# A chunked attention and a wave MLP: two stages in sequence, and the same work woven by pairs of batches

## The chip, the cores and the metric

The kernel runs on one core of a Trainium2 chip. Its engines have instruction queues of their own: TensorE (PE, and PEld for its weight loads) for matmuls and transposes, VectorE (DVE), ScalarE (ACT), GpSimd (POOL) and SyncE (SP). POOL issues the transfers that load the inputs, SP those that store the output; both run on the same 16 DMA engines. The metric is the device time of one execution in microseconds (us), and a version's time is the median of its runs.

## What is computed

```python
# q, k, v: (8, 8, 576, 64); w_theta, w_ch: (512, 512); w_tok_r, w_tok_i: (576, 576); float32
q_c, k_c, v_c = (t.reshape(B, H, 9, 64, D) for t in (q, k, v))      # chunks of 64 tokens
attn = softmax(q_c @ k_c.T / sqrt(64))                              # inside a chunk only
x = (attn @ v_c) -> (B, S, H * D)                                   # (8, 576, 512)
theta = x @ w_theta
zr, zi = x * cos(theta), x * sin(theta)
y[b] = w_tok_r @ zr[b] + w_tok_i @ zi[b]                            # over the tokens of a batch
u = x + y
out = u + maximum(u @ w_ch, 0.0)
```

The softmax's subtraction of the row's maximum leaves its value unchanged; both kernels leave it out. Inputs become 16-bit floats (f16) as they are loaded, sums are 32-bit, the output is 32-bit.

## The kernel before

A batch has 576 tokens: four tiles of 128 and one of 64 (`SB_SZ`). In every loop over tiles the fifth pass works on half a tile.

**Weights.** POOL loads `w_theta` and `w_ch` as they are; both token weights are loaded and then transposed on TensorE (line 78, 25 blocks each), since the token mix contracts over the tokens.

**Attention, a loop over 8 batches.** POOL issues 15 loads a batch (line 107): q, k and v for each of 5 tiles, 128 KB each as written, 64 KB for the half tile; the buffers hold two batches. q and k are transposed per tile and pair of heads (line 120) and copied out by DVE (lines 127, 130). Per head, TensorE computes 9 blocks of 64x64 scores (line 142), ACT takes the exponential of the first eight and the ninth chunk in two instructions (lines 147, 153), and 9 matmuls with a column of ones give the row sums (line 161). Then values times weights (line 180), and DVE multiplies by the reciprocal sums (lines 167, 185) into `x16`, of which there is one for each batch.

**MoE part, a second loop over 8 batches.** x is transposed (line 202; ACT copies, line 207), theta is computed per tile (line 219), ACT takes cosine and sine (lines 226, 230), DVE the products zr and zi (lines 234, 237). The token mix takes the transposed token weights as the stationary and z as the moving operand, so that its result `ps_y` has tokens on the partitions: 5 output tiles of 10 matmuls each, 512 columns wide (line 251). DVE adds x (line 259). u is transposed again (line 269; ACT copies, line 274), multiplied with `w_ch` (line 282), and DVE computes max(., 0) + u in one instruction (line 290) into one of two output buffers, which SP stores.

All PSUM tiles come from one pool of 8 buffers, one bank each. The framework's scheduler chooses each engine's order from the program's order and from what is ready.

## Time and profile before

| | |
|---|---|
| runs | 331.72 us median of 3 (331.07 to 333.35) |
| span of the profiled execution | 329.0 us |
| median of the runs less that span | 2.7 us |
| TensorE busy (x matmuls) | 285.2 us (x3138) |
| DVE, ACT, POOL busy | 146.2, 115.7, 105.4 us |
| loads | 120 issues for q, k, v; 16.54 MB written in all by POOL's queue |
| stores | 40 issues, 9.44 MB |

An instruction's busy time runs from its start to its modelled end, and matmuls overlap: the sum of busy times is no measure of the pace. The pace is the time from one start to the next. In the slices of the page each digit is a share in tenths; PEclk is the granted clock of TensorE, where 9 stands for the full one. A load's size in the profile is what it writes (16-bit); it reads twice as much.

### The profile page before, as it was taken

How to read it: one execution, taken by the hardware profiler on the slowest of the kernel's cores; microseconds unless marked ns; L12 is line 12 of the kernel's file. 1: busy time of each engine (PE TensorE's matmuls, PEld its weight loads, DVE VectorE, ACT ScalarE, POOL GpSimd, SP SyncE). 2: the span in 40 equal slices, each digit the busy share in tenths (PEclk: the TensorE clock that was granted, in tenths of full speed). 3: DMA queues.
4: the chain of work that ended last, by engine and by line, in shares of the span. 5: the costliest groups of instructions: out<-in, count | busy, mean ns of one | idle time of the engine just before them, and what ended most of it. 6: DMA issues, size and time to landing. Idle time of an engine off the chain costs nothing.

```text
span 329.0 us, 7260 instructions
## 1 busy us (share of the span) xinstructions
PE 285.2 (87%) x3138; PEld 159.2 (48%) x3138; DVE 146.2 (44%) x319; ACT 115.7 (35%) x290; POOL 105.4 (32%) x132
## 2 busy tenths in 40 slices
PE   0328977879869889999999999999999999999992
PEld 0216866768858777334344344344344344344340
DVE  0216437357347354544534625525535534533532
ACT  0001440431421424805615515425426326227220
POOL 8189999999999900000000000000000000000000
PEclk9999577575676576999999999999999999999998
DMA  6999999999999980003003004004004003003004
GB/s 107 175 134 152 146 138 138 149 142 140 151 138 144 147 44 3 2 0 130 16 0 131 16 0 140 5 0 145 0 0 146 0 0 131 14 1 129 15 1 144
DMA packets 120064, 26.44 MB, mean 80 GB/s; under 512 B 113248, under 2 KB 115424, under 8 KB 120032
## 3 DMA queue, kind: packets, MB, share of 16 engines
q0 software_dynamic: 114784, 16.54, 79.4%
q1 hardware_dynamic: 5248, 9.44, 8.4%
q8 instruction: 24, 0.39, 0.5%
q14 instruction: 8, 0.07, 0.1%
HBM read 33.06 MB, written 9.44 MB: 129 GB/s over the span
## 4 chain that ended last, share of the span: by engine, by line
PE 62%; POOL 14%; DMA 12%; DVE 7%; issue 2%; ACT 1%; DVEq 0%; POOLq 0%; ACTq 0%
PE ps_y L251 30%; POOL qk L107 9%; PE ps_theta L219 8%; PE ps_uw L282 8%; DMA out_dram<-o 5%; POOL v L107 5%; DMA wtok_nat<-in_moe_w_tok_r_dram 3%; PE ps_uT L269 3%; PE ps_sT L142 3%; PE ps_xT L202 2%; PE ps_rs L161 2%; PE ps_wtokT L78 2%; DVE o L290 2%; DMA wtok_nat<-in_moe_w_tok_i_dram 2%; DMA qk<-in_q_dram 2%
## 5 line engine op out<-in xcount | busy, mean ns | idle before, releaser
L251 PE MATMUL ps_y<-zr,wtokTr 128*128 128x512 f16 (+3 forms) x200 | 53.9, 382 | 0.7 <-DVE zr L234 0.6
L251 PE MATMUL ps_y<-zi,wtokTi 128*128 128x512 f16 (+3 forms) x200 | 54.5, 384 | 0.0
L259 DVE TENSOR_TENSOR u<-ps_y,x 128x512 f16<-128x512 f32 (+1 forms) x40 | 27.6, 690 | 53.6 <-PE ps_y L251 53.6
L147 ACT ACTIVATE eT<-ps_sT 128x256 f16<-128x256 f32 x64 | 24.4, 382 | 69.5 <-PE ps_sT L142 66.7
L274 ACT COPY uT<-ps_uT 128x512 f16<-128x512 f16 (+1 forms) x40 | 18.6, 564 | 82.3 <-PE ps_uT L269 82.3
L290 DVE SCALAR_TENSOR_TENSOR o<-ps_uw,u 128x512 f32<-128x512 f32 (+1 forms) x40 | 27.6, 690 | 40.0 <-DMA out_dram<-o 22.5
L107 POOL DMA_DIRECT2D v<-in_v_dram x40 | 37.3, 933 | 1.5 <-DMA wch<-in_moe_w_ch_dram 1.3
L107 POOL DMA_DIRECT2D qk<-in_q_dram x40 | 37.3, 933 | 1.2 <-issue 0.8
L219 PE MATMUL ps_theta<-wtheta,xT 128*128 128x512 f16 (+1 forms) x160 | 36.9, 381 | 0.7 <-ACT xT L207 0.7
L107 POOL DMA_DIRECT2D qk<-in_k_dram x40 | 37.3, 932 | 0.1
L282 PE MATMUL ps_uw<-wch,uT 128*128 128x512 f16 (+1 forms) x160 | 36.9, 381 | 0.0
L251 PEld LDWEIGHTS <-wtokTi 128*128 128x128 f16 (+3 forms) x200 | 16.5, 99 | 38.5 <-issue 29.3
L120 PE MATMUL ps_qkT<-id,qk 128*128 128x128 f16 (+1 forms) x320 | 29.9, 267 | 5.8 <-DMA qk<-in_q_dram 4.5
L142 PE MATMUL ps_sT<-qT,kT 64*64 64x64 f16 x576 | 30.1, 232 | 3.7 <-DVE kT L130 3.6
L251 PEld LDWEIGHTS <-wtokTr 128*128 128x128 f16 (+3 forms) x200 | 17.8, 99 | 31.9 <-issue 17.0
L161 PE MATMUL ps_rs<-ones,eT 64*64 64x1 f16 x576 | 26.9, 191 | 7.0 <-ACT eT L147 7.0
L120 PEld LDWEIGHTS <-qk 128*128 128x128 f16 (+1 forms) x320 | 26.1, 127 | 8.7 <-DMA qk<-in_q_dram 6.1
L230 ACT ACTIVATE sin<-ps_theta,zerob 128x512 f16<-128x512 f32 (+1 forms) x40 | 29.6, 741 | 0.0
L226 ACT ACTIVATE cos<-ps_theta,pihalf 128x512 f16<-128x512 f32 (+1 forms) x40 | 29.5, 737 | 0.0
L207 ACT COPY xT<-ps_xT 128x512 f16<-128x512 f16 (+1 forms) x40 | 18.6, 564 | 28.2 <-PE ps_xT L202 28.2
L161 PEld LDWEIGHTS <-eT 64*64 64x64 f16 x576 | 21.8, 144 | 11.1 <-ACT eT L147 8.9
L185 DVE TENSOR_TENSOR x<-ps_xout,recip 128x512 f16<-128x512 f32 (+1 forms) x40 | 24.6, 681 | 0.4
(39 smaller groups left out, 242.2 us busy)
## 6 DMA issues: line engine op xcount, KB each, us to landing
out_dram<-o SPq DMA_DIRECT2D x32, 256.0 KB, 2.0
qk<-in_q_dram POOLq DMA_DIRECT2D x32, 128.0 KB, 5.5
qk<-in_k_dram POOLq DMA_DIRECT2D x32, 128.0 KB, 5.8
v<-in_v_dram POOLq DMA_DIRECT2D x32, 128.0 KB, 5.8
out_dram<-o SPq DMA_DIRECT2D x8, 128.0 KB, 2.3
wtok_nat<-in_moe_w_tok_r_dram POOLq DMA_DIRECT2D x1, 576.0 KB, 10.0
wtok_nat<-in_moe_w_tok_i_dram POOLq DMA_DIRECT2D x1, 576.0 KB, 6.1
wtheta<-in_moe_w_theta_dram POOLq DMA_DIRECT2D x1, 512.0 KB, 6.1
```

Source lines behind the costliest of these rows:

```text
L107: nc.gpsimd.dma_start(dst, t_ap[b, :, sb * P : sb * P + ns, :].rearrange("h s d -> s h d"),)
L120: nc.tensor.transpose(pqk[:, which, e, 0:ns], qk16[0:ns, sb, which, 2 * e : 2 * e + 2, :].rearrange("s h d -> s (h d)"), id16[0:ns, 0:ns],)
L142: nc.tensor.matmul(pst[cp * CH : cp * CH + CH, cb, :], kT[par * D : par * D + D, e, sl], qT[par * D : par * D + D, e, sl],)
L161: nc.tensor.matmul(ps_rs[cp * CH : cp * CH + CH, cb, h : h + 1], eT[cp * CH : cp * CH + CH, h, cb, :], ones16[cp * CH : cp * CH + CH, :],)
L185: nc.vector.tensor_tensor(out=x16[b][0:ns, sb, :].rearrange("s (h d) -> s h d", h=H), in0=psx[0:ns], in1=recip[0:ns, sb, :].unsqueeze(-1). ...
L219: nc.tensor.matmul(pth[0:ns], xT[:, db, sb * P : sb * P + ns], wtheta16[:, db, :], start=(db == 0), stop=(db == NDB - 1),)
L226: nc.scalar.activation(out=cos16[0:ns, sb, :], in_=pth[0:ns], func=AF.Sin, bias=pihalf[0:ns], scale=1.0,)
L230: nc.scalar.activation(out=sin16[0:ns, sb, :], in_=pth[0:ns], func=AF.Sin, bias=zerob[0:ns], scale=1.0,)
L251: nc.tensor.matmul(psy[0:nt], wT[0:ns, sb, tsl], z[0:ns, sb, :], start=(step == 0), stop=(step == nsteps - 1),)
L259: nc.vector.tensor_tensor(out=u16[0:nt, mt, :], in0=psy[0:nt], in1=x16[b][0:nt, mt, :], op=ALU.add,)
L282: nc.tensor.matmul(puw[0:nt], uT[:, db, mt * P : mt * P + nt], wch16[:, db, :], start=(db == 0), stop=(db == NDB - 1),)
L290: nc.vector.scalar_tensor_tensor(out=o32[0:nt], in0=puw[0:nt], scalar=0.0, in1=u16[0:nt, mt, :], op0=ALU.max, op1=ALU.add,)
```

## The change

Two batches are one pair of 1152 tokens, that is 9 full tiles; tile 4 (`MID`) holds the last 64 tokens of the first and the first 64 of the second batch. `GROUPS` puts the 9 tiles into steps of 2, 2, 1, 2 and 2. A PSUM tile is now two banks, and there are 4 of them.

- The loads for tile 4 go in two halves. q and k have 6 buffers of one tile, v has room for two pairs, with a 65th column of ones behind each head.
- `a1` transposes q and k (one DVE copy a group), `a2` computes scores (one exponential a group), `a3` multiplies with values and ones at once, so that the row sum comes out as the 65th column, `a4` transposes x, `a5` computes theta, cosine, sine and the products. For tile 4, half of zr and zi is exchanged between partitions by two transfers that SP issues, so that one tile holds both parts of one batch.
- `y` is the token mix transposed: z is the stationary operand and the token weights move, 288 columns at a time, 18 matmuls for each of 4 channel blocks of a batch. Its result has channels on the partitions, and DVE adds the transposed x: this is already the transposed u. The token weights are transposed twice (`tok_w`): for the first batch of a pair, and for the second with rows shifted by 64.
- `w` multiplies by `w_ch`, and by the identity to get u back in its natural layout; ACT takes the relu, DVE the sum, SP stores. The output has 4 buffers.
- The order is written out (`manual_schedule`): each engine takes its instructions in the program's order. `weave` spreads the steps of a second list evenly between those of a first. While pair p goes through `y` and `w`, pair p + 1 goes through `a1` to `a5`, and POOL issues its loads.

The core of the diff; what it removes are the two loops above.

```diff
+def weave(main, filler):
+    n, m = len(main), len(filler)
+    done = 0
+    for i, step in enumerate(main):
+        step()
+        want = ((i + 1) * m) // n
+        while done < want:
+            filler[done]()
+            done += 1
...
-    psum = ctx.enter_context(tc.tile_pool(name="psum", bufs=8, space=bass.MemoryType.PSUM))
+    GROUPS = [(0, 2), (2, 2), (4, 1), (5, 2), (7, 2)]
+    psum = ctx.enter_context(
+        tc.tile_pool(name="psum", bufs=4, space=bass.MemoryType.PSUM)
+    )
+    nat = ctx.enter_context(tc.tile_pool(name="nat", bufs=6))
+    ctx.enter_context(tc.manual_schedule())
...
+    def tok_ranges(j):
+        if j < MID:
+            return [(0, 0, j * P, P)]
+        if j > MID:
+            return [(0, 1, j * P - S, P)]
+        return [(0, 0, MID * P, CH), (CH, 1, 0, CH)]
+    def load_qk(p, j):
+        t = nat.tile([P, 2, H, D], FP16, name="qk16")
+        nats[p, j] = t
+        for ti, ap in enumerate((q, k)):
+            for pp, bb, s0, n in tok_ranges(j):
+                nc.gpsimd.dma_start(
+                    t[pp : pp + n, ti],
+                    ap[2 * p + bb, :, s0 : s0 + n, :].rearrange("h s d -> s h d"),
+                )
...
+    def tok_w(par, kt):
+        ps = psum2("ps_wT", FP16)
+        for tb in range(KT + 1):
+            nt = P if tb < KT else CH
+            if kt < 2 * KT:
+                s0 = (kt % KT) * P + (CH if par else 0)
+                parts = [(slice(0, P), kt // KT, s0)]
+            else:
+                s0 = 0 if par else KT * P
+                parts = [(slice(ri * CH, ri * CH + CH), ri, s0) for ri in range(2)]
+            for rows, ri, s0 in parts:
+                nc.tensor.transpose(
+                    ps[rows, tb * P : tb * P + nt],
+                    wnat[0:nt, tb, ri, s0 : s0 + rows.stop - rows.start],
+                    id16[0:nt, 0:nt],
+                )
+        if kt % 2:
+            nc.vector.tensor_copy(out=wT[par][:, kt, :], in_=ps[:, 0:S])
+        else:
+            nc.scalar.copy(out=wT[par][:, kt, :], in_=ps[:, 0:S])
...
+    def a1(p, g):
+        j0, n = GROUPS[g]
+        ps = psum2("ps_qkT", FP16)
+        psv = ps.rearrange("p (w e s) -> p w e s", w=2, e=NE)
+        for jj in range(n):
+            t = nats.pop((p, j0 + jj))
+            for w in range(2):
+                for e in range(NE):
                     nc.tensor.transpose(
+                        psv[:, w, e, jj * P : jj * P + P],
+                        t[:, w, 2 * e : 2 * e + 2, :].rearrange("s h d -> s (h d)"),
+                        id16,
                     )
+        qkT = qkp.tile([P, 2, NE, 2 * P], FP16, name="qkT")
+        st[p]["qkT"][g] = qkT
+        nc.vector.tensor_copy(
+            out=qkT[:, :, :, 0 : n * P], in_=psv[:, :, :, 0 : n * P]
+        )
+    def a2(p, g):
+        j0, n = GROUPS[g]
+        qkT = st[p]["qkT"].pop(g)
+        ps = psum2("ps_sT")
+        psv = ps.rearrange("p (r j e c) -> p r j e c", r=2, j=2, e=NE)
+        for jj in range(n):
+            for e in range(NE):
+                for par in range(2):
+                    for cp in range(2):
+                        sl = slice(jj * P + cp * CH, jj * P + cp * CH + CH)
+                        nc.tensor.matmul(
+                            psv[cp * CH : cp * CH + CH, par, jj, e, :],
+                            qkT[par * D : par * D + D, 1, e, sl],
+                            qkT[par * D : par * D + D, 0, e, sl],
                         )
+        eT = epool.tile([P, 2, NE, 2, CH], FP16, name="eT")
+        st[p]["eT"][g] = eT
+        nc.scalar.activation(
+            out=eT[:, 0:n].rearrange("p j e r c -> p r (j e) c"),
+            in_=psv[:, :, 0:n].rearrange("p r j e c -> p r (j e) c"),
+            func=AF.Exp,
+            scale=scale,
+        )
+    def a3(p, j, g):
+        j0, n = GROUPS[g]
+        eT = st[p]["eT"][g]
+        slot = (p % 2) * NT + j
+        ps = psum2("ps_x")
+        psv = ps.rearrange("p (f c) -> p f c", f=2)
+        for h in range(H):
+            hf, h4 = h // NE, h % NE
+            for cp in range(2):
+                sl = slice(cp * CH, cp * CH + CH)
+                nc.tensor.matmul(
+                    psv[sl, hf, h4 * (D + 1) : (h4 + 1) * (D + 1)],
+                    eT[sl, j - j0, h // 2, h % 2, :],
+                    v16[sl, slot, h, 0 : D + 1],
+                )
+        px = psv[:, :, 0 : NE * (D + 1)].rearrange("p f (h c) -> p f h c", h=NE)
+        recip = trig.tile([P, 2, NE, 1], FP32, name="recip")
+        nc.vector.reciprocal(out=recip, in_=px[:, :, :, D : D + 1])
+        nc.vector.tensor_tensor(
+            out=st[p]["x"][:, j, :].rearrange("s (f h d) -> s f h d", f=2, h=NE),
+            in0=px[:, :, :, 0:D],
+            in1=recip.broadcast_to((P, 2, NE, D)),
+            op=ALU.mult,
+        )
...
+    def a5(p, g):
+        j0, n = GROUPS[g]
+        ps = psum2("ps_theta")
+        for jj in range(n):
+            j = j0 + jj
+            for db in range(NDB):
+                nc.tensor.matmul(
+                    ps[:, jj * DM : jj * DM + DM],
+                    st[p]["xT"][:, db, j * P : j * P + P],
+                    wtheta16[:, db, :],
+                    start=(db == 0),
+                    stop=(db == NDB - 1),
+                )
+        cos = trig.tile([P, 2, DM], FP16, name="cos16")
+        sin = trig.tile([P, 2, DM], FP16, name="sin16")
+        pin = ps[:, 0 : n * DM]
+        nc.scalar.activation(
+            out=cos[:, 0:n].rearrange("p a e -> p (a e)"), in_=pin,
+            func=AF.Sin, bias=pihalf, scale=1.0,
+        )
+        nc.scalar.activation(
+            out=sin[:, 0:n].rearrange("p a e -> p (a e)"), in_=pin, func=AF.Sin
+        )
+        x, zr, zi = st[p]["x"], st[p]["zr"], st[p]["zi"]
+        if n == 2:
+            nc.vector.tensor_mul(
+                zr[:, j0 : j0 + n], x[:, j0 : j0 + n], cos[:, 0:n]
+            )
+            nc.vector.tensor_mul(
+                zi[:, j0 : j0 + n], x[:, j0 : j0 + n], sin[:, 0:n]
+            )
+            return
+        lo, hi = slice(0, CH), slice(CH, P)
+        tmp = trig.tile([P, DM], FP16, name="zmid")
+        nc.vector.tensor_mul(zr[lo, j0], x[lo, j0], cos[lo, 0])
+        nc.vector.tensor_mul(tmp[lo], x[lo, j0], sin[lo, 0])
+        nc.vector.tensor_mul(zi[hi, j0], x[hi, j0], sin[hi, 0])
+        nc.vector.tensor_mul(tmp[hi], x[hi, j0], cos[hi, 0])
+        nc.sync.dma_start(zr[hi, j0], tmp[lo])
+        nc.sync.dma_start(zi[lo, j0], tmp[hi])
+    def y(p, bb, db):
+        s = st[p]
+        if bb == 0 and db == 0:
+            s["uT"] = pairp.tile([P, NDB, T], FP16, name="uT")
+        first = bb * (MID + 1)
+        kts = [(kt, s["zr"] if kt < KT else s["zi"], first + kt % KT)
+               for kt in range(2 * KT)]
+        kts.append((2 * KT, s["zi"] if bb else s["zr"], MID))
+        ps = psum2("ps_y")
+        psv = ps.rearrange("p (f c) -> p f c", f=2)
+        for i, (kt, z, j) in enumerate(kts):
+            for hf in range(2):
+                nc.tensor.matmul(
+                    psv[:, hf, 0:HS],
+                    z[:, j, db * P : db * P + P],
+                    wT[bb][:, kt, hf * HS : hf * HS + HS],
+                    start=(i == 0),
+                    stop=(i == 2 * KT),
+                )
+        sl = slice(bb * S, bb * S + S)
+        nc.vector.tensor_tensor(
+            out=s["uT"][:, db, sl].rearrange("p (f c) -> p f c", f=2),
+            in0=psv[:, :, 0:HS],
+            in1=s["xT"][:, db, sl].rearrange("p (f c) -> p f c", f=2),
+            op=ALU.add,
+        )
+    def w(p, j):
+        uT = st[p]["uT"]
+        ps = psum2("ps_uw")
+        for db in range(NDB):
+            nc.tensor.matmul(
+                ps[:, 0:DM],
+                uT[:, db, j * P : j * P + P],
+                wch16[:, db, :],
+                start=(db == 0),
+                stop=(db == NDB - 1),
+            )
+            nc.tensor.matmul(
+                ps[:, DM + db * P : DM + db * P + P],
+                uT[:, db, j * P : j * P + P],
+                id16,
+            )
+        r = outp.tile([P, DM], FP32, name="relu", bufs=3)
+        nc.scalar.activation(out=r, in_=ps[:, 0:DM], func=AF.Relu)
+        o = outp.tile([P, DM], FP32, name="o32")
+        nc.vector.tensor_tensor(out=o, in0=ps[:, DM : 2 * DM], in1=r, op=ALU.add)
+        for pp, bb, s0, n in tok_ranges(j):
+            nc.sync.dma_start(out[2 * p + bb, s0 : s0 + n, :], o[pp : pp + n])
...
+    def front(p, gs):
+        steps = [c(a1, p, gs[0])]
+        for i, g in enumerate(gs):
+            if i + 1 < len(gs):
+                steps.append(c(a1, p, gs[i + 1]))
+            steps.append(c(a2, p, g))
+        return steps
+    def back(p, gs):
+        steps = []
+        for i in range(len(gs) + 2):
+            if i < len(gs):
+                j0, n = GROUPS[gs[i]]
+                steps += [c(a3, p, j, gs[i]) for j in range(j0, j0 + n)]
+            if 0 <= i - 1 < len(gs):
+                steps.append(c(a4, p, gs[i - 1]))
+            if 0 <= i - 2 < len(gs):
+                steps.append(c(a5, p, gs[i - 2]))
+        return steps
+    new_pair(0)
+    for j in range(MID + 1):
+        load_qk(0, j)
+        load_v(0, j)
+    load_w(moe_w_theta, wtheta16)
+    load_tok_w()
+    for j in range(MID + 1, NT):
+        load_qk(0, j)
+        load_v(0, j)
+    load_w(moe_w_ch, wch16)
+    for f in front(0, [0, 1, 2]):
+        f()
+    weave(back(0, [0, 1, 2]), [c(tok_w, 0, kt) for kt in range(2 * KT + 1)])
+    for p in range(NP):
+        more = p + 1 < NP
+        if more:
+            new_pair(p + 1)
+            load_pair(p + 1)
+        y0 = [c(y, p, 0, db) for db in range(NDB)]
+        y1 = [c(y, p, 1, db) for db in range(NDB)]
+        ws = [c(w, p, j) for j in range(NT)]
+        nxt = list(range(NG))
+        if p == 0:
+            weave(
+                y0,
+                front(0, [3, 4]) + back(0, [3, 4])
+                + [c(tok_w, 1, kt) for kt in range(2 * KT + 1)],
+            )
+            weave(y1, front(p + 1, nxt))
+            weave(ws, back(p + 1, nxt))
+            continue
+        if more:
+            weave(y0, front(p + 1, nxt))
+        else:
+            weave(y0, [])
+        main = []
+        for db in range(NDB):
+            main += [y1[db], ws[db]]
+        main += ws[NDB:]
+        weave(main, back(p + 1, nxt) if more else [])
```

287 lines of the change are left out of this document (62 added, 225 removed).

## Prediction, made before the changed kernel ran

> **What bounds the kernel now.** I read the page's slices first, then the chain that ended last.
>
> ```profile
> span 329.0 us, 7260 instructions
> ...
> PE   0328977879869889999999999999999999999992
> ...
> POOL 8189999999999900000000000000000000000000
> PEclk9999577575676576999999999999999999999998
> DMA  6999999999999980003003004004004003003004
> ```
>
> One slice is 8.2 us. There are two programs, one behind the other. In slices 2 to 14 POOL and the DMA engines are full, and TensorE is busy in pieces at a lowered clock; from slice 17 POOL and DMA are idle and TensorE is full. No slice has both full. The chain in order of time gives the second half; this is batch 2 of 8:
>
> ```profile
> 177.03 1.22 PE ps_xT L202 x20
> 178.25 4.54 PE ps_theta L219 x20
> 182.79 12.60 PE ps_y L251 x50
> 195.39 1.22 PE ps_uT L269 x20
> 196.61 4.54 PE ps_uw L282 x20
> ```
>
> These five follow each other without a gap: 24.12 us a batch, 193 us for eight, all TensorE. Ahead of them lie about 128 us that the loads pace, and behind them the last stores. The next rows price the loads:
>
> ```profile
> 1.27 0.90 POOL L63 DMA_DIRECT2D wtheta<-in_moe_w_theta_dram  x1 [0.33 <-issue]
> ...
> 44.09 0.90 POOL L107 DMA_DIRECT2D v<-in_v_dram  x1
> 44.96 0.91 POOL L107 DMA_DIRECT2D qk<-in_q_dram  x1
> ...
> 50.15 0.77 POOL L107 DMA_DIRECT2D qk<-in_q_dram  x1
> 50.82 0.78 POOL L107 DMA_DIRECT2D qk<-in_k_dram  x1
> ```
> ```profile
> GB/s 0 5 73 207 201 207 185 200 164 155 155 112 27 156 201 163 155 155 154 153 145 152 144 150 144 146 149 120 111 145 159 145 149 147 157 146 108 127 152 151
> ```
> ```profile
> DMA to landing us min/median/max: 4.7/5.8/10.3
> ```
>
> A full load (128 KB) is issued every 0.87 us, a half one (64 rows) every 0.67. The second fence is the rate in the first 60 us, 1.5 us a step: weights move at about 200 GB/s, q, k and v at about 150, which is 128 KB in 0.87 us; issue and engines are level. The third is q and k's time from issue to landing.
>
> **What the change removes, adds and moves.** The loads stay 120 of the same shapes (a middle tile of 64+64 rows stands for two half tiles): per pair 24 x 0.87 + 6 x 0.67 = 25 us. They now run beside TensorE's work for the pair before. So the sum is TensorE's work, plus the start that nothing covers, plus bubbles, plus the end.
>
> TensorE's price by columns: 4.54/20 = 227 ns at 512 columns, 1.22/20 = 61 ns at a mean of 115.2 (16 of 128, 4 of 64). The line through both has 0.418 ns a column: 66 ns at 128, 133 ns at 288. The token mix pays more, 12.60/50 = 252 ns; what it has and theta has not are ten matmuls with 64 rows of weights a batch, so each of these costs (12.60 - 50 x 0.227)/10 = 0.125 us extra. For 288 columns the bounds are 128 ns (proportional to 512) and 142 (proportional to 252); I take 133.
>
> Per pair of batches, after:
> - token mix, 144 matmuls x 133 = 19.2 us (before 2 x 12.60 = 25.2; no partial tile is left in it)
> - theta, 36 x 227 = 8.2 (before 9.1)
> - output product 36 x 227 = 8.2, and 36 identity matmuls in place of the transposes of u, x 66 = 2.4: 10.6 (before 11.5)
> - x transposed, 36 x 66 = 2.4
>
> That is 40.4 against 48.2. The attention's matmuls, as they run now:
>
> ```profile
> 120.97 0.42 PE L142 MATMUL ps_sT<-qT,kT 64*64 64x64 f16 x24
> ```
> ```profile
> 125.22:127.16 1.94, 1.94 (x67) 0.50 0.00 0
> ```
>
> The second row is a window: its length, TensorE's busy time and count, granted clock, DMA. Transposes of q and k: 72 x 66 = 4.8. Scores: 24 in 0.42 us bound one at 18 ns; with a matmul's own 0.2 us of latency off it is 9. At 12: 144 x 12 = 1.7. Values times weights: 1.94/67 = 29 ns at clock 0.50, so between 15 and 29 at full clock and 65 columns; at 20: 2.9. The 576 row sums by matmul go, for one more column in these. Each of the 5 + 9 steps with 64x64 weights now stands between full-array work; at 0.125 us each 1.8 (bounds 0 and, if entering and leaving each cost that, 3.5). [...]
>
> So a pair is 40.4 + 4.8 + 1.7 + 2.9 + 1.8 = 51.6, four are 206.4. The token weights are transposed twice, straight and shifted by half a tile: 100 x 66 = 6.6. TensorE: **213 us**.
>
> **The start.** Ahead of the first token mix come tiles 0 to 4 of pair 0 (12 full and 6 half issues, 14.5 us from 1.3 to 15.8), then w_theta and both token weights, 1.85 MB. Their data follow those of the loads (which are about 3 us behind their issue) and take 9.3 us at 200 GB/s: about 28, landed by 29. The order is fixed, so TensorE stands at the fifth transposed token block until then, as it does today:
>
> ```profile
> 23.43 3.65 PE L78 MATMUL ps_wtokT<-id,wtok_nat 128*128 128x128 f16 x25 [6.40 <-DMA wtok_nat<-in_moe_w_tok_i_dram]
> ```
>
> Behind it come 30 transposes (2.0), 20 theta matmuls (4.5), 4 transposes (0.3), and some 2 us for a low clock at first: the token mix starts at **38** (34 to 42). Done by then: 5/9 of 20.0 us of attention and theta, 8 switches, 50 token transposes: 15.4. Left: 213 - 15.4 = 197.6.
>
> **What hides the rest.** ACT and DVE work by start-to-start times:
>
> ```profile
> 201.57 2.33 ACT L207 COPY xT<-ps_xT 128x512 f16<-128x512 f16 x5 [3.43 <-PE ps_xT L202]
> 203.75 0.74 ACT L226 ACTIVATE cos<-ps_theta,pihalf 128x512 f16<-128x512 f32 x1
> 204.33 0.73 ACT L230 ACTIVATE sin<-ps_theta,zerob 128x512 f16<-128x512 f32 x1
> ```
> ```profile
> 113.53 0.14 DVE L170 RECIPROCAL recip<-ps_rs 64x8 f32<-64x8 f32 x1
> 113.72 3.07 DVE L185 TENSOR_TENSOR x<-ps_xout,recip 128x512 f16<-128x512 f32 x5
> ...
> 117.71 0.41 DVE L130 COPY kT<-ps_qkT 128x512 f16<-128x512 f16 x1
> 118.04 0.41 DVE L127 COPY qT<-ps_qkT 128x512 f16<-128x512 f16 x1
> ```
> ```profile
> 278.74 0.34 DVE zi L237
> 279.08 0.33 DVE zr L234
> ```
> ```profile
> L147 ACT ACT_TABLE_LOAD x1 | 1.3, 1283 | 24.0 <-DMA wtok_nat<-in_moe_w_tok_i_dram 24.0
> L226 ACT ACT_TABLE_LOAD x1 | 1.3, 1283 | 0.0
> ```
>
> ACT per pair, in units of 512 columns: exp 9 x 0.58, copies 9 x 0.47, cos and sin 18 x 0.58, the new relu 9 x 0.58, two table loads: 27. DVE: q and k 18 x 0.33, reciprocal and product 9 x (0.14 + 0.62), zr and zi 18 x 0.34, the mix's sums 8 x 0.7, outputs 9 x 0.69: 31. Both lie beside 51.6 of TensorE. In the tightest stage (outputs woven with values, x and theta: TensorE 24.9) they have 21 and 20, so cover is thin there. If it is gone, ACT's excess is paid directly.
>
> Bubbles, where a step waits for its forerunner: the middle tile's two on-chip copies by DMA ahead of the first mix, 2 us; pair 0's second half, whose attention follows step on step, 2.5; after each of three q/k/score blocks the last scores wait for a copy of 4 x 0.33, 1.2 each; the tightest stage three times, 1.3 each. Six buffers for q and k make the loads of a pair's tiles 6 to 8 wait until its first transposes free them. POOL then stands with v and all later loads behind it; 8 issues and a landing, 7 + 4.7 = 11.7, face about 10.7 of TensorE's work up to their use: 1 each, 3 times. Together 15 (0 to 45).
>
> The end, from the last output's DVE to the span's end, is 329.0 - 325.6 today:
>
> ```profile
> 324.94 0.68 DVE L290 SCALAR_TENSOR_TENSOR o<-ps_uw,u 64x512 f32<-64x512 f32 x1 [1.30 <-DMA out_dram<-o]
> ```
>
> 3.4, with relu and sum ahead of it 4.8. **Sum: 38 + 197.6 + 15 + 4.8 = 255.4 of span.** The median of the runs, 331.72, is 2.7 above today's span: **258 us**.
>
> **Rivals.**
> - *Everything overlaps.* No bubbles, values at 15 ns, switches half price: 258 - 15 - 3 - 3 = 237. For it: the load is below TensorE's on every engine.
> - *Four PSUM buffers in one fixed order couple the engines.* Before has eight. Each step holds its buffer until ACT or DVE is done, and the fifth step waits. Were the bubbles three times as long: 288. For it: 21 of 24.9 us leaves little slack in a stage with bursts of cos and sin.
> - *The clock.* The other side of no change. The clock is granted by stretches:
>
> ```profile
> 26.10:29.50 3.40, 3.40 (x31) 3.10 (x31) 2.44 (x9) 0.00 (x0) 3.12 (x4) 1.00 2.41 153
> 29.50:32.90 3.40, 1.91 (x28) 1.26 (x25) 2.10 (x7) 0.42 (x2) 3.40 (x5) 1.00 3.33 150
> 32.90:43.20 10.30, 9.78 (x239) 9.04 (x239) 5.46 (x14) 3.35 (x15) 9.52 (x12) 0.50 2.99 138
> ```
>
> A stretch of transposes (26.1 to 29.5) is followed by full clock; scores with gaps (29.5 to 32.9) by half clock, though TensorE is 95% busy in the third row. If small steps and short waits among the mix keep it low, 197.6/c replaces 197.6. It turns slower than today when 197.6/c > 197.6 + 74, c below 0.73; at the 0.65 of the attention today the time is 258 + 106 = 364. Against it: at least half of every woven stage is 128-row matmuls, and from slice 17 on such work ran at full clock. Were only the three mix-and-scores blocks (16 us each) at 0.65: 284. [...]
> - *Loads still pace.* The change would then not do what it says: stores and loads share the engines, and the six-buffer ring costs 10 us a pair rather than 1: 285. Against it: 25 us of loads in 52.
> - *relu and sin in different tables.* In the tightest stage they alternate: some 9 loads x 1.28, three times, less the 4 us of slack each: 258 + 23 = 281. The trace has two loads in all, with Copy among both, and no relu. [...]
>
> **How the numbers follow.** Forecast 0.60 (244 to 272); all overlapped 0.12; coupled 0.15; the clock in part 0.05, throughout 0.02; loads 0.03; tables 0.02; no gain at all 0.01. Unknown prices stretch the forecast by 14 down and 16 up (values, switches, 288 columns, the start), so the range is 238 to 288. A change within 1% can't be told from none here: faster 0.97, same 0.01, slower 0.02.
>
> **What would show it.** PEclk full from slice 6 on and PE at 9 there; POOL and DMA busy in blocks of about 25 us, four times; the mix at 133 ns a matmul; the first mix at 38; about 52 us from one pair's first mix to the next, 40 for the last. I am wrong if the mix pays for 576 weight loads that its shorter matmuls do not hide, if TensorE waits long for ACT in the outputs' stage, or if the clock stays low.

## The result, and the profile after

| | before | after |
|---|---|---|
| median of 4 runs | 331.39 us (329.94 to 333.35) | 251.41 us (250.76 to 254.23) |
| span of the profiled execution | 329.0 us | 249.6 us |
| ratio after/before | | 0.759, 95% interval 0.754 to 0.765 |

The forecast was 258 us in a range of 238 to 288. Medians from here on leave out a run that is over 1.5% above the fastest of its kernel (four runs in all, in three of the experiments), ranges show every run. The page of the changed kernel, first its slices (one is now 6.24 us):

```profile
PE   0362779287899978789997999999989999999993
...
POOL 9997496098106998400699940005600000000000
PEclk9999999779999999999999999999999999999998
```

The loads stand in blocks in POOL's row, and from slice 5 on TensorE is at 7 or above in every slice but the eighth and the last: loads and mix run at once. The clock, at 5 to 7 tenths in nearly a third of the old span, reads full but for slices 8 and 9 and the last. The same by stretches, with cuts at the starts of the four pairs' token mixes (length; busy time and count of TensorE, its weight loads, DVE, ACT, POOL; granted clock, DMA share, GB/s):

```profile
41.75:48.60 6.85, 2.12 (x16) 1.46 (x15) 2.46 (x6) 2.83 (x4) 0.07 (x1) 0.84 1.74 128
48.60:52.70 4.10, 4.06 (x38) 3.71 (x42) 1.98 (x2) 0.00 (x0) 2.27 (x3) 0.50 0.20 13
...
117.80:168.10 50.30, 47.99 (x650) 32.93 (x649) 31.55 (x53) 25.76 (x32) 25.13 (x30) 1.00 1.27 122
168.10:217.90 49.80, 48.06 (x651) 33.06 (x649) 31.69 (x53) 25.89 (x32) 7.88 (x9) 1.00 0.52 76
217.90:249.60 31.70, 27.38 (x216) 19.38 (x214) 14.38 (x21) 7.60 (x12) 0.00 (x0) 0.97 0.21 76
```

From one pair's first mix to the next it takes 50 us, at full clock; the first of the two full stretches shown has 25.1 us of load issues inside it. Ahead of them, from pair 0's first mix to pair 1's, it takes 76 us (41.75 to 117.80), since pair 0's second half and the second set of transposed token weights lie there too. The first two rows above are the one bad place, and the chain of work that ended last says what it is:

```profile
43.48 5.03 DMA zr<-zmid
...
49.28 3.43 PE ps_qkT L177 x32
...
164.68 3.45 PE ps_theta L262 x16
...
170.34 1.79 PE ps_qkT L177 x32
...
174.33 0.38 PE ps_sT L199 x32
...
186.49 0.37 PE ps_x L224 x16
...
217.86 11.03 PE ps_y L313 x90
...
245.31 0.61 ACT relu L346
```

Pair 0's middle tile waits for the on-chip exchange of zr and zi. The clock then falls to half, and 32 transposes take 3.43 us where the same 32 take 1.79 a few stages on. The other rows give the prices that were estimated: 56 ns for a matmul of 128 columns (1.79/32), 122.6 for 288 (11.03/90), 215.6 for 512 (3.45/16), 12 for a score block, 23 for a block of values. Each step with 64x64 weights also pays for the change of shape. TensorE's timeline shows it at eight transposes between two steps of scores:

```profile
174.64 0.62 PE L177 MATMUL ps_qkT<-id,qk 128*128 128x128 f16 x8
175.19 0.44 PE L199 MATMUL ps_sT<-qkT 64*64 64x64 f16 x32
```

From start to start they take 0.55 us, where 8 x 56 ns are 0.45: 0.10 for going into the scores. Coming out costs 0.10 to 0.11 by the starts of single matmuls in the same trace, and is part of the 12 and 23 ns.

TensorE's waits between 50 and 249 us (us in total, times, longest):

```profile
PE ps_sT L199 <- DVE qkT L184: 3.6, 4, 0.9
PE ps_xT L246 <- DVE x L232: 2.0, 5, 0.5
PE ps_uw L333 <- ACT sin L276: 1.8, 4, 1.0
PE ps_uw L333 <- DVE x L232: 1.2, 4, 0.4
PE ps_y L313 <- ACT sin L276: 1.0, 1, 1.0
PE ps_qkT L177 <- DMA qk<-in_k_dram: 1.0, 2, 0.6
PE ps_theta L262 <- DVE x L232: 0.7, 2, 0.5
```

11.3 us in 200, none over 1 us: from there to the end it is TensorE's own work that takes most of the time. The output product (`ps_uw`) reads neither the sines nor x, so that its 3.0 us behind these are waits for a PSUM buffer.

### The profile page after: what moved, and what is told of

It is laid out like the page before. It is cut to its first block, busy times and chain, and to the rows that moved or that the text cites. A ratio compares the mean times of both kernels' runs of the same rounds, so it can differ in the third digit from the quotient of the medians.

```text
span 249.6 us, 6130 instructions
## 1 busy us (share of the span) xinstructions
PE 209.2 (84%) x2692; PEld 144.3 (58%) x2692; DVE 130.5 (52%) x217; ACT 111.8 (45%) x136; POOL 105.8 (42%) x133
## 3 DMA queue, kind: packets, MB, share of 16 engines
q1 hardware_dynamic: 5888, 9.96, 11.6%
## 4 chain that ended last, share of the span: by engine, by line
PE 53%; POOL 11%; DMA 10%; DVE 10%; ACT 10%; issue 5%; POOLq 0%
PE ps_y L313 21%; PE ps_theta L262 9%; PE ps_uw L333 9%; POOL qk L109 7%; DMA qk<-in_k_dram 4%; ACT sin L276 4%; PE ps_qkT L177 4%; DMA wnat<-in_moe_w_tok_r_dram 4%; DVE x L232 4%; POOL v L117 3%; PE ps_xT L246 3%; ACT cos L272 2%; PE ps_x L224 2%; PE ps_wT L145 2%; PE ps_uw L340 2%
## 5 line engine op out<-in xcount | busy, mean ns | idle before, releaser
L313 PE MATMUL ps_y<-wT,zr 128*128 128x288 f16 x288 | 42.8, 287 | 6.1 <-DMA zr<-zmid 4.8
L321 DVE TENSOR_TENSOR uT<-ps_y,xT 128x576 f16<-128x576 f32 x32 | 24.2, 756 | 41.4 <-PE ps_y L313 41.4
L333 PE MATMUL ps_uw<-wch,uT 128*128 128x512 f16 x144 | 42.6, 380 | 3.0 <-ACT sin L276 1.8
L206 ACT ACTIVATE eT<-ps_sT 128x1024 f16<-128x1024 f32 (+1 forms) x20 | 18.4, 938 | 54.6 <-PE ps_sT L199 54.6
L313 PE MATMUL ps_y<-wT,zi 128*128 128x288 f16 x288 | 40.5, 286 | 0.0
L262 PE MATMUL ps_theta<-wtheta,xT 128*128 128x512 f16 x144 | 33.7, 379 | 2.4 <-ACT sin L276 1.7
L313 PEld LDWEIGHTS <-zr 128*128 128x128 f16 x288 | 26.7, 98 | 14.1 <-issue 6.3
L313 PEld LDWEIGHTS <-zi 128*128 128x128 f16 x288 | 28.2, 98 | 7.1
L348 DVE TENSOR_TENSOR o<-ps_uw,relu 128x512 f32<-128x512 f32 x36 | 24.8, 688 | 13.4 <-ACT relu L346 13.1
L340 PE MATMUL ps_uw<-id,uT 128*128 128x128 f16 x144 | 31.5, 219 | 0.0
L232 DVE TENSOR_TENSOR x<-ps_x,recip 128x512 f16<-128x512 f32 x36 | 24.9, 691 | 1.2
L272 ACT ACTIVATE cos<-ps_theta,pihalf 128x1024 f16<-128x1024 f32 (+1 forms) x20 | 20.6, 1029 | 9.8 <-PE ps_theta L262 9.8
## 6 DMA issues: line engine op xcount, KB each, us to landing
wnat<-in_moe_w_tok_i_dram POOLq DMA_DIRECT2D x1, 576.0 KB, 11.3
```

What stands on the lines that cost most here:

```text
L232: nc.vector.tensor_tensor(out=st[p]["x"][:, j, :].rearrange("s (f h d) -> s f h d", f=2, h=NE), in0=px[:, :, :, 0:D], in1=recip.broadcast_ ...
L262: nc.tensor.matmul(ps[:, jj * DM : jj * DM + DM], st[p]["xT"][:, db, j * P : j * P + P], wtheta16[:, db, :], start=(db == 0), stop=(db == ...
L272: nc.scalar.activation(out=cos[:, 0:n].rearrange("p a e -> p (a e)"), in_=pin, func=AF.Sin, bias=pihalf, scale=1.0,)
L313: nc.tensor.matmul(psv[:, hf, 0:HS], z[:, j, db * P : db * P + P], wT[bb][:, kt, hf * HS : hf * HS + HS], start=(i == 0), stop=(i == 2 * KT),)
L321: nc.vector.tensor_tensor(out=s["uT"][:, db, sl].rearrange("p (f c) -> p f c", f=2), in0=psv[:, :, 0:HS], in1=s["xT"][:, db, sl].rearrange ...
L333: nc.tensor.matmul(ps[:, 0:DM], uT[:, db, j * P : j * P + P], wch16[:, db, :], start=(db == 0), stop=(db == NDB - 1),)
```

## The experiments

My theory: about half of the gain is cheaper TensorE work and half is the attention laid beside the MoE part; what is left beyond TensorE's sum is the start, the exchange and the thin cover of four PSUM buffers. Rivals: the order alone does it, or the weaving matters less than the new shapes. Every ratio below is against runs of the kernel before on the same chip, whose medians were 331.1 to 331.8 us.

**All attention first, then the changed MoE part (no overlap at all).** The edit, abridged and in words where it is long:

```diff
     for p in range(NP):
         new_pair(p)
+        load_pair(p); front and a3 of pair p      # token weights' transposes woven in
+    for p in range(NP):
+        new_moe(p); a4, a5, y, w of pair p, step after step
-            weave(y0, front(p + 1, nxt))
-        weave(main, back(p + 1, nxt) if more else [])
```

> The changed kernel with its overlap undone: the same steps, tiles and matmuls, but the attention of all four pairs comes first (weights loaded ahead of it), then transposes of x, theta, mix and output pair by pair, nothing woven, one buffer each for xT, zr, zi and uT. Theory (the gain is the loads running beside the second half, with the cheaper matmuls as the smaller part): about 118 us paced by the loads, then 4 x 37 us of TensorE work plus some 4 us of waits a pair and the end: 280 to 295. Rival (the cheaper matmuls brought nearly all, the overlap little): 255 to 265.

Measured 295.12 us (294.87 to 295.52), ratio 0.890 (0.887 to 0.894): 0.1 us above the theory's range. The chain and a slice row of this kernel:

```profile
140.71 17.64 PE ps_y L317 x144
180.92 17.64 PE ps_y L317 x144
```
```profile
POOL 9487999999799998000000000000000000000000
```

POOL is idle from slice 17 (of 7.3 us) on, and the first mix comes at 140.7: the two programs stand one behind the other again. A pair takes 40.2 us from mix to mix, where two batches took 48.24, which for four is 32 of the 36 us gained; a mix matmul costs 122.5 ns with nothing between. So new shapes give 36 us, and the remaining 44 of the 80 (295.1 to 251.4) come from laying the attention's loads and work beside the MoE part. The split holds for this order of the steps: a pair's MoE steps aren't woven among themselves here either, and TensorE waits 8.8 us in all for ACT's copies of x, which the weaving hides as well.

**The overlap without the weaving: each stage runs its main steps, then the other pair's.**

```diff
     for i, step in enumerate(main):
         step()
-        want = ((i + 1) * m) // n
-        while done < want:
-            filler[done]()
-            done += 1
+    for step in filler:
+        step()
```

> The changed kernel with the steps not woven: a pair's mix and outputs first, then the next pair's attention and theta, one behind the other; loads still run ahead beside them. Theory (weaving hides the chains from engine to engine; TensorE's work is the same): a front alone is paced by DVE's copies, a back alone by ACT's cosines and sines and DVE's products, 3 to 6 us a pair: 260 to 272. Rival (four PSUM buffers let the engines run ahead anyway, only the loads' overlap matters): 250 to 254. Second rival (every step's chain lies open, some 0.7 us for 46 steps a pair): over 320.

Measured 287.23 us (286.94 to 290.82), ratio 0.869 (0.863 to 0.875): outside every range given. Its clock by slices, and TensorE's longest waits between 60 and 285 us:

```profile
PEclk9999999988955977999858997999958997999999
```
```profile
PE ps_qkT L175 <- DMA qk<-in_q_dram: 8.3, 6, 2.2
PE ps_qkT L175 <- DMA qk<-in_k_dram: 6.6, 7, 2.6
```

I had counted only ACT's and DVE's lag. What I missed is that a fixed order also sets when a buffer comes free. The six q and k buffers are emptied by the transposes, these now come in one block after the mix, and the loads of tiles 6 to 8 can start only then: 14.9 us of waits for q and k in these rows, and the clock row dips to 5 at three places, once for each pair that is loaded beside another's mix. Without weaving, and with these waits, loads beside the mix gain only 8 us over the kernel with no overlap (295.12 to 287.23).

**The same with nine buffers for q and k, and with the exchange done by DVE** (the next experiment but one has it by itself).

```diff
-    nat = ctx.enter_context(tc.tile_pool(name="nat", bufs=6))
+    nat = ctx.enter_context(tc.tile_pool(name="nat", bufs=9))
```

> The kernel with the steps not woven, with nine in place of six buffers for q and k and the middle tile's exchange by DVE. It splits the 36 us that weaving is worth. Theory (most of them are the ring of six, whose loads for tiles 6 to 8 then lie open with a fall of the clock behind them: TensorE waits 16 us for q and k beyond the start in that kernel's trace, and the stretches at half clock cost some 6): 257 to 265. Rival (most of it is the chain from engine to engine inside a front and a back): 274 to 283.

Measured 263.67 us (262.36 to 267.79; 266.02 with all four runs), ratio 0.796 (0.789 to 0.803): in the theory's range, 10 us below the rival's. Of the 21 to 24 us to the last experiment some 5 are the exchange, so 16 to 19 were the ring of buffers: the 14.9 in its waits and the low clock behind them. The woven kernel with the same two edits takes 245.28 (below): weaving itself is worth 18 to 21 us, and in the changed kernel it also hides that the ring is short.

**Three PSUM buffers in place of four.**

```diff
-        tc.tile_pool(name="psum", bufs=4, space=bass.MemoryType.PSUM)
+        tc.tile_pool(name="psum", bufs=3, space=bass.MemoryType.PSUM)
```

> The changed kernel with three PSUM buffers of two banks in place of four. Theory (the buffers couple the engines, and a good part of TensorE's idle time in the stage of outputs is a wait for a buffer): half as many bubbles again to twice as many, 10 to 20 us slower than the changed kernel, 261 to 272. Rival (the fixed order and the data's own chains make the idle time, buffers do not): 251 to 254.

Measured 260.62 us (259.81 to 263.75; 262.11 with all four runs), ratio 0.788 (0.782 to 0.794), at the lower edge of the coupling theory's range and far from the rival's. Four of TensorE's waits between 50 and 258 us:

```profile
PE ps_uw L333 <- DVE o L348: 3.6, 5, 0.9
PE ps_x L224 <- ACT sin L276: 3.1, 4, 1.3
PE ps_uw L333 <- DVE x L232: 2.7, 4, 1.1
PE ps_uw L333 <- DVE uT L321: 2.2, 4, 0.9
```

These four are 11.6 us; of them only the third stands in the changed kernel's list, with 1.2. They are steps that wait for a buffer which DVE or ACT still reads. All of TensorE's waits in that stretch come to 20.0 us against 11.3, and the two profiled spans are 9.3 us apart (258.9 and 249.6). Whether more buffers than four, or eight of one bank, would gain wasn't tried.

**The exchange by DVE: the product is written straight to the other half of the partitions.**

```diff
-        tmp = trig.tile([P, DM], FP16, name="zmid")
-        nc.vector.tensor_mul(tmp[lo], x[lo, j0], sin[lo, 0])
-        nc.vector.tensor_mul(tmp[hi], x[hi, j0], cos[hi, 0])
-        nc.sync.dma_start(zr[hi, j0], tmp[lo])
-        nc.sync.dma_start(zi[lo, j0], tmp[hi])
+        nc.vector.tensor_mul(zr[hi, j0], x[lo, j0], sin[lo, 0])
+        nc.vector.tensor_mul(zi[lo, j0], x[hi, j0], cos[hi, 0])
```

> The changed kernel with the middle tile's exchange done by DVE, which writes two of its four products straight to the other half of the partitions, in place of two transfers issued by SP. Theory (the first mix waits 4.8 us for the transfer, and the clock falls to half after it, which costs another 1.7): 4 to 7 us faster than the changed kernel, 244.5 to 247.5. Rival (behind the transfer the loads of tiles 5 to 8 are late as well, or the four products take as long): within 1 us of the changed kernel, 250 to 252.

Measured 246.63 us (245.55 to 247.55), ratio 0.744 (0.740 to 0.748): as expected, 4.8 us less than the changed kernel. TensorE's timeline at the same place, first of the changed kernel, then of this one:

```profile
41.75 1.14 PE L313 MATMUL ps_y<-wT,zr 128*128 128x288 f16 x8 [0.30 <-ACT sin L276]
...
48.64 0.64 PE L313 MATMUL ps_y<-wT,zr 128*128 128x288 f16 x2 [4.78 <-DMA zr<-zmid]
49.08 3.62 PE L177 MATMUL ps_qkT<-id,qk 128*128 128x128 f16 x32
```
```profile
44.56 0.41 PE L310 MATMUL ps_y<-wT,zr 128*128 128x288 f16 x2
44.81 1.95 PE L177 MATMUL ps_qkT<-id,qk 128*128 128x128 f16 x32
```

Without the transfer the wait of 4.78 us is gone and the transposes behind it run at full clock: 1.7 us more. (The profiled first mix of this kernel came 0.9 us later, at 42.61, and its clock row stands at 8 in slice 15, from 86.0 to 92.2 us, so the two profiled spans are only 3.8 us apart.)

**Nine buffers for q and k in the woven kernel with DVE's exchange** (the edit as above).

> The changed kernel with the exchange done by DVE and nine in place of six buffers for q and k, so that a pair's loads never wait for its first transposes. Against the kernel with the DVE exchange alone (246.6): theory (the ring costs about 1 us in each of three blocks of scores): 243.5 to 245.5. Rival (the ring is hidden behind the mix): 246 to 247.5.

Measured 245.28 us (243.57 to 245.91), ratio 0.739 (0.735 to 0.743), against 246.63 with six: the intervals overlap, so the time doesn't settle it. In the trace the waits for k (two in the changed kernel, 1.0 us together) are gone.

**Before, with the half tiles of the mix side by side.** The prediction charged ten matmuls of 64 weight rows with 0.125 us each, as the price of changing the shape. Taking the imaginary tiles in reverse puts the two half tiles next to each other: fewer changes, as many matmuls. The edit, abridged:

```diff
-                for wT, z in ((wtokT_r, zr16), (wtokT_i, zi16)):
-                    for sb in range(NSB):
+                for wT, z, sb in ([(wtokT_r, zr16, s) for s in range(NSB)]
+                    + [(wtokT_i, zi16, s) for s in reversed(range(NSB))]):
```

> The kernel before with one order changed: in its token mix the two blocks with 64 rows of weights stand next to each other, so that TensorE goes once rather than twice a tile from 128-row to 64-row weights and back. Theory (what costs is the going over and back): 40 changes fewer x 0.125 to 0.18 us, 5 to 7 us faster than before, 324 to 327. Rival (a matmul with 64 rows is itself dear): no difference, 330.5 to 332.5.

Measured 327.95 us (327.56 to 329.0), ratio 0.989 (0.985 to 0.993): between both. The chain of this kernel, then TensorE's timeline at one pair of half tiles:

```profile
207.30 12.21 PE ps_y L254 x50
```
```profile
236.48 0.38 PE L254 MATMUL ps_y<-zi,wtokTi 128*128 128x512 f16 x1
236.79 0.39 PE L254 MATMUL ps_y<-zr,wtokTr 64*128 64x512 f16 x1
237.01 0.38 PE L254 MATMUL ps_y<-zi,wtokTi 64*128 64x512 f16 x1
...
237.32 0.39 PE L254 MATMUL ps_y<-zi,wtokTi 128*128 128x512 f16 x1
```

From start to start it is 0.31 us into the first matmul with 64 rows, 0.22 to the second, 0.31 back to 128 rows. At 0.216 for a full one the change costs 0.10 us each way, and a matmul with 64 rows costs no more than a full one: the theory's mechanism holds and the rival's doesn't. The gain is smaller than the theory's because fewer changes went. The traces of both kernels have about 17 changes a batch before (some half tiles stand side by side there already) and between 13 and 14 here, which brings 12.60 to 12.21. At full-tile price the 50 would take 10.78 (50 x 215.6 ns), and 17 changes at 0.10 are 1.7 of the 1.82 above that. The 0.125 of the prediction was this cost of changes, spread over ten matmuls.

**Before, with the row sums as a 65th value column**, and PSUM split into 4 buffers of one bank and 2 of two (abridged):

```diff
-                    nc.tensor.matmul(ps_rs[...], eT[...], ones16[...])
+            nc.vector.memset(v16[:, :, :, D : D + 1], 1.0)
-    psum = ctx.enter_context(tc.tile_pool(name="psum", bufs=8, ...))
+    psum = ctx.enter_context(tc.tile_pool(name="psum", bufs=4, ...))
```

> One part of the change alone in the kernel before: a column of ones behind each head's values gives the row sums, and the 576 matmuls for them go (26.9 us of TensorE's busy time); four one-bank PSUM buffers and two of two banks. Theory (the attention half is paced by the loads, so TensorE's work there is covered; only the last batch's is not): 329.5 to 332. Rival (TensorE's queue is on the path there, as its share of the chain suggests): 321 to 327.

Measured 345.54 us (344.94 to 346.13), ratio 1.044 (1.039 to 1.048): a miss. Its chain:

```profile
159.62 4.59 PE ps_theta L217 x20
...
183.54 1.65 ACT xT L205 x3
185.24 4.59 PE ps_theta L217 x20
```

ACT's copies now stand in the chain of the MoE part, whose batch takes 25.6 us instead of 24.12: with four buffers the fifth transposed block waits for a copy (5.1 us of TensorE's waits for ACT's copies of x, eight of them). Eight batches make 12 of the 14 us lost. That was my split of PSUM, not the column, so it was run again with eight one-bank buffers, two of them for the values of a tile:

> The kernel before with the row sums as a 65th value column, now with its eight one-bank PSUM buffers kept (each tile's values go to two of them, four heads each). The run with four small and two large buffers was 14 us slower than before; in its trace the attention half ended no earlier, and each MoE batch took 25.7 rather than 24.1 us, since transposes waited for copies. Theory (the row sums are covered by the loads and worth nothing; the 14 us were the four buffers): 329.5 to 332. Rival (the 65 columns themselves cost time in the attention half): 335 to 345. Second rival (the row sums were on the path): 321 to 327.

Measured 331.8 us, ratio 1.002 (1.000 to 1.005): no difference. The 576 row sums lay beside work that the loads pace; taking them out is worth nothing there. (DVE has 431 instructions for 319 in this version, so it is the sum of both edits that comes to nothing.)

**The start reordered** (on top of DVE's exchange): token weights and `w_theta` loaded ahead of q, k and v, all 100 token transposes first, then pair 0's first five tiles through every step as they land (abridged).

```diff
-    for j in range(MID + 1):
-        load_qk(0, j)
-        load_v(0, j)
...
+    load_pair(0)
...
+    tok_w(par, kt) for all kt, par          # ahead of everything
+    c(a1, 0, 0), c(a2, 0, 0), c(a1, 0, 1), c(a3, 0, 0, 0), ..., c(a5, 0, 2)
```

> The changed kernel with the DVE exchange and another start: the token weights and w_theta are loaded first, all 100 token transposes stand ahead of the attention, and pair 0's first five tiles go through all their steps as they land. The bytes ahead of the first mix are the same. Theory (from 26 us on the start is TensorE's pile of transposes, theta and values behind the last load; done while waiting, it costs nothing): the first mix at 31 to 34 rather than 41.8, half of the token transposes out of the next stage, 10 to 13 us faster than the DVE exchange alone: 233 to 237. Rival (the start is paced by the loads; tiles 5 to 8, which now land at 37, hold the next stage up by what was won): 243 to 247.

Measured 245.24 us (244.2 to 246.94), ratio 0.740 (0.736 to 0.744): missed by 8 us, and no faster than with DVE's exchange alone, whose runs it overlaps. The number lies in the rival's range, but not for the rival's cause: the first mix itself came late, and the stage behind it was shorter than before. TensorE's and ACT's timelines:

```profile
7.52 12.89 PE L145 MATMUL ps_wT<-id,wnat 128*128 128x128 f16 x100 [7.52 <-DMA wnat<-in_moe_w_tok_r_dram]
...
38.16 0.44 PE L224 MATMUL ps_x<-v,eT 64*64 64x65 f16 x16 [3.23 <-ACT eT L206]
...
45.72 1.14 PE L310 MATMUL ps_y<-wT,zr 128*128 128x288 f16 x8
```
```profile
31.07 1.28 ACT L272 ACT_TABLE_LOAD   x1
...
36.22 1.28 ACT L206 ACT_TABLE_LOAD   x1
```

The first mix comes at 45.72, later than the 42.61 of the order it replaces. The transposes took 129 ns each, not 56, and exponentials now alternate with sines, so ACT reloads its tables between them and TensorE waits for it. What makes up for it is the next stage, which has 50 transposes less: from pair 0's first mix to pair 1's it is 66.1 us in this trace (45.72 to 111.78), against 71.0 with DVE's exchange alone (42.61 to 113.59).

**Two more on top of it.** Nine buffers, and the steps that make q, k and scores placed between the mix steps one by one (abridged; `spread` is a new function that writes the order in its comment):

```diff
-            weave(y1, front(p + 1, nxt))
+            spread(y1, front(p + 1, nxt))    # fr[0:2] y[0] fr[2:5] y[1] fr[5:7] y[2] fr[7:9] y[3] fr[9]
```

> DVE exchange, the other start, nine buffers for q and k, and in the blocks of mix and scores the mix's step behind the transposes of the next group, so that the last scores have 2.2 us of mix ahead of them rather than a wait for DVE's copy. Theory (the gains add up: ring 1 to 3 us, last scores 0.9 us in three blocks): 228 to 234. Rival (what is won in these blocks is lost to the stage behind them, which has ACT as its limit): the same as the other start alone, within 1 us.

Measured 239.77 us (239.34 to 243.95; 240.5 with all four runs), ratio 0.724 (0.720 to 0.728): 5.5 us less than the reordered start alone, but above the range since the start hadn't paid. Then with all of pair 0's first exponentials ahead of its first sine:

```diff
-        c(a2, 0, 1), c(a4, 0, 0), c(a1, 0, 2), c(a3, 0, 2, 1), c(a3, 0, 3, 1),
-        c(a5, 0, 0), c(a2, 0, 2), c(a4, 0, 1), c(a3, 0, 4, 2), c(a5, 0, 1),
+        c(a2, 0, 1), c(a4, 0, 0), c(a3, 0, 2, 1), c(a3, 0, 3, 1), c(a4, 0, 1),
+        c(a1, 0, 2), c(a2, 0, 2), c(a5, 0, 0), c(a3, 0, 4, 2), c(a5, 0, 1),
```

> The best so far (240.5) with pair 0's first exponentials all ahead of its first sine. In the trace of the other start the first mix came at 45.7, not at 31 to 34: with sines between the exponentials ACT changed tables four times, and the middle tile's exponential, values and x waited behind cosines and sines. Theory (that order was the start's limit): the first mix at 35 to 38, 231 to 235. Rival (the transposes and values at half clock are the limit): 239 to 241.5.

Measured 238.12 us (237.85 to 238.57), ratio 0.719 (0.716 to 0.722), between the two ranges. The first mix still starts late:

```profile
35.23 3.52 PE L262 MATMUL ps_theta<-wtheta,xT 128*128 128x512 f16 x8
...
44.43 1.14 PE L310 MATMUL ps_y<-wT,zr 128*128 128x288 f16 x8
```

So the order of exponentials and sines was worth 1.3 us of the first mix (45.72 to 44.43). The rival has its part: eight theta matmuls took 3.52 us here, where the changed kernel's took 1.89 at 37.74 us. It is the fastest version: 13.3 us less than the changed kernel, 93 less than before. What a good start would be stays open: two orders tried both left the first mix behind the changed kernel's 41.75.

## Why the prediction was right, and where its steps were off

258 was forecast and 251.4 measured, 6.6 apart. The mechanism is the one forecast: the loads go beside the MoE part, and TensorE's own work is what remains. That the number is so near is partly luck. The span was 255.4 against 249.6; the other 0.8 is the time around the span, 1.8 us (251.4 - 249.6) where I took 2.7, having set a median against the span of another run. Inside the span larger errors cancel:

| term | predicted | measured | how |
|---|---|---|---|
| first token mix | 38 | 41.75 | timeline |
| TensorE's work from there | 191.6 | 177.5 | counts x the prices above |
| waits and changes of shape | 15 + 6 | 26 | the rest of the span |
| end | 4.8 | 4.3 | relu at 245.31 to 249.6 |

**TensorE's work, -14.** The 177.5 are mix 576 x 122.6, theta 124 x 215.6, outputs 144 x (215.6 + 56), transposes 124 + 248 + 50 at 56, scores 496 x 12 and values 496 x 23 ns. The step that was off is the price line by columns. I drew it through 20 theta matmuls and 20 transposes of the kernel before, of which four each work on a half tile; what those pay for two changes of shape (4.54 us against 20 x 215.6 ns is 0.23 more) entered the line as 12.8 ns on every matmul. The measured prices lie on 0.416 ns a column and 2.8 ns besides. The page counts a weight load for every matmul (2692 of each), and the streams keep these prices with them: the mix, at 122.6 ns, doesn't pay for its 576. The 0.2 us that the prediction took off 24 scores is the length of a lone one in the trace of the kernel before: 0.21, at 120.08 us.

**The first mix, +3.75.** The weights did arrive before the 29 us that I gave. TensorE's timeline of the changed kernel from there:

```profile
26.32 0.77 PE L145 MATMUL ps_wT<-id,wnat 128*128 128x128 f16 x5 [5.97 <-DMA wnat<-in_moe_w_tok_r_dram]
27.02 0.65 PE L224 MATMUL ps_x<-v,eT 64*64 64x65 f16 x16
```

They landed at 26.3; but the work behind them took 15.45 us (26.3 to 41.75) and not 9. The values and the transposes of x stood there too, five transposes took 0.70 us where 0.28 is the full-clock price, which the 2 us set aside for a low clock didn't cover, and TensorE waited 2.0 us for the sines. I had added TensorE's durations, and this is a chain through three engines.

**Waits, +5.** The exchange cost 4.8 rather than 2, then 1.7 for the lowered clock, which I had not counted; the experiment that removes it gives 4.8 back. The waits in the table above are 11.3: the last scores wait 0.9 a block (1.2 forecast), the waits for x and the sines are the thin cover of the tightest stage and the four buffers, and the ring of q and k costs 1.0 in two blocks (forecast 1 in each of three). That makes 17.8 of 26. The other 8 lie where TensorE counts as busy. Read from start to start in the trace, 4.4 of them are the last matmul ahead of each wait, which counts as busy to its modelled end, and most of the rest are changes of shape: 77 of them from the first mix on, 7.7 us at 0.10 each, part of which the 12 and 23 ns hold. The forecast's 6 (48 steps at 0.125) was the right order of size, from a wrong split: 0.125 for a step with 64x64 weights, where going in and out costs 0.2, but steps that follow each other pay once.

**The rest of the forecast.** Pair periods were 50.3 and 49.8 (52), but 76.05 for pair 0, whose own second half and 50 token transposes I had left out of that sign, and 31.7 for the last, where I had said 40: its theta and its transposes of x, 10.6 of my 40.4, are done a period earlier. As reckoned came 25.1 us of issues a pair (25), DVE 31.6 and ACT 25.8 (31 and 27). The clock rival fell: 1.00 in both full pairs, and full in slices 10 to 39, where I had said from 6 on. TensorE's row isn't at 9 from slice 6 on, as I had said, but between 7 and 9, and at 2 in the eighth. The loads rival fell with 1.0 us of waits for k. The table rival fell: the groups have five table loads before exponentials (L206), five before cosines (L272) and none before relu:

```profile
L206 ACT ACT_TABLE_LOAD x5 | 6.4, 1283 | 0.8 <-PEq L439 0.7
L272 ACT ACT_TABLE_LOAD x5 | 6.4, 1283 | 0.1
```

The coupling rival was near: one buffer fewer costs 9.2 us. "Everything overlaps" (237) did not happen, though the fastest version comes to 238.

## What to carry to other kernels

Before two stages are woven, sum the engine that will bound them, at prices taken from full tiles only with the changes of shape counted apart, and add what starts it as a chain, not as a sum. In a fixed order, ask of every ring of buffers which instruction frees a buffer and where the order puts it: six buffers cost about 1 us when woven and 16 to 19 when not. A short wait on the bounding engine can cost more than its length (here 4.8 us, and 1.7 more at the clock of 0.50 behind it), so a small transfer on the path is worth replacing even by work on a busy engine.

## What the runs showed of the hardware that I had not expected

The same 64 KB on-chip transfer took between 1.9 and 5.0 us. The view of the tile `zmid` of the changed kernel gives them over the four pairs, from issue to landing:

```profile
DMA to landing us min/median/max: 1.9/1.9/5.0
```

The 5.0 is pair 0's, which moves while the loads of the next tiles run (DMA share 1.52 from the first issue of the two transfers to the last landing); the others had little beside them (0.37 to 0.38). DVE wrote its result to the other half of the partitions at no extra time: 0.42 us for such a product in the trace of the kernel with DVE's exchange, as for `zmid` in the changed kernel's.

The clock row can read full where the pace is half: TensorE's 100 token transposes of the reordered start took 129 ns each from 7.52 us on, and the page gives full clock there. The full-width ones of q and k behind them start 107 ns apart (16 take 1.89 us and 12 take 1.46), and 56 later on (32 in 1.95). The changed kernel's trace has no entry for the clock before 32.7 us, and its row reads full there too, so there the row says nothing. The time from start to start is the surer sign.

It also leaves open what raises the clock. The prediction read from the kernel before that a stretch of transposes can: there full clock is on record from 29.5 us, behind 6.1 us of transposes alone (from 23.43 on). In the reordered start nothing but transposes ran from 7.5 to 22 us, and the last 16 of them still kept the pace of 107 ns.

Two steps with differently shaped weights cost TensorE about 0.10 us at the change, in either direction, both between 128 and 64 rows (0.31 us where a full one takes 0.216) and between full and 64x64 weights (0.55 for eight transposes ahead of scores, where 8 x 56 ns are 0.45). A matmul with 64 rows of weights took 0.22 us, what a full one does.
